# A fixed queue planned anew, with GpSimd left out of casts and copies of global values from tile 6 on

## The chip, the cores and the metric

The kernel runs on one core of a Trainium2 chip. The metric is the time of the device for one execution in microseconds (us), the median of several runs. An engine has its own queue and works through it in order: TensorE (PE in the profile; its weight loads are PEld), VectorE (DVE), ScalarE (ACT), GpSimd (POOL) and SyncE (SP), which here only issues DMA transfers.

## The reference: what is computed

Inputs are q, k and v of shape (4, 8, 768, 64), that is 4 batches, 8 heads, 768 positions and 64 columns, and four weights in float32. First comes attention with a narrow window, 96 local positions and 8 global ones, and then a feed-forward network (FFN) with three first matrices:

```python
scores = scale * q @ k.T                          # per batch and head
is_global = pos[None, :] < n_global               # 8
is_local = (rel >= 0) & (rel < n_local)           # 96, rel = query - key
bias = -slopes[h] * where(is_global & ~is_local, n_local, abs(rel))
a = softmax(where(is_global | is_local, scores + bias, -1e9))
x = (a @ v) as 3072 rows of 512                   # 4*768 rows, 8 heads * 64
h = maximum(maximum(x @ w1, x @ w2), x @ w3)      # 768 columns
out = h @ w_out                                   # 3072 x 512
```

## The kernel before

The 3072 rows are 24 *tiles* T of 128 rows, six per batch. A pair of tiles is a *group* G (256 rows), in which q, k and v are loaded. For the FFN the tiles form seven *chunks* of 4, 2, 2, 4, 4, 4 and 4 tiles, so a matmul has 512 or, in chunks 1 and 2, 256 columns.

Attention needs only the tile's own keys and those of the tile before it. The window is shorter than a tile, so the first rows of the tile before are free when it has been used as own tile, and the keys and values of the 8 global positions are copied into them: G(T) copies global keys, V(T) global values. V(T) stands behind the product of tile T that read these rows and ahead of the product of tile T+1. It has two halves, on partitions 0 to 3 and 64 to 67, one for even and one for odd positions.

All work is cut into *units*. A string, SCHEDULE, holds them in one order, and the kernel issues them one by one in that order; each engine thus gets its queue. A tile framework adds the semaphore waits where a unit reads what another wrote or takes a buffer that another used. A unit is a letter, its numbers, and, behind @, the buffer slot that it takes; where a unit may run on several engines the last number tells which: 0 ScalarE, 1 VectorE, 2 GpSimd, 3 a DMA. The letters:

- `l` a load of q (l0), k (l1) or v (l2) of a group, issued by SyncE (lines 213 and 220); group 12 stands for four tiles of batch 0 at once. `c` the cast of q or k to bfloat16 (L185), on GpSimd in two halves; `v` the cast of half a tile of v (L238). `w`, `W`, `q`, `Q` load and cast the FFN weights.
- `x`, `y` a transpose of q or k by TensorE (L252, L258) and its copy out of PSUM (L266, L269); `X` the same by a DMA transpose that SyncE issues (L274). `G` (L289, L291) and `V` (L302 on GpSimd, four-byte words; L304 on the others), as above.
- `S` the scores of four heads (L324; L316 adds the bias by a matmul where the unit's last number is 1), `e` the exponential (L331), `m` the multiplication by the mask and bias factor where S added no bias (L340; L342 for a batch's first tile), `A` the product with v (L366, L369) with the softmax sums as a 65th column, `n` the normalisation, a reciprocal and a multiplication (L377, L378). `B` and `K` write the eight heads' bias and mask tables from `R`.
- `t`, `u` the transpose of a normalised tile by TensorE (L393) and its copy (L396); `Z` the same by a DMA transpose (L399).
- `F` one FFN group c.f.j: four matmuls (L408) for chunk c, columns f (six times 128), matrix j. `f` takes it out of PSUM: j=0 a copy (L422, ScalarE or VectorE), j=1 a maximum (L424) and j=2 a maximum (L427), both on VectorE.
- `O`, `o`, `s` one output tile: six matmuls (L432), the copy out of PSUM (L447) and the store (L451). `E` is the last chunk's output (L437, L438). `D` are matmuls of zeros that fill waits at the start (L507).

PSUM has eight banks. F, O, t and x take one, S and A two, and the next unit on a bank waits until the last reader of the one before is done. So VectorE, which empties most banks, and TensorE are coupled both ways. The Vector, Scalar and Gpsimd units are picked from one table:

```python
copies = (nc.scalar.copy, nc.vector.tensor_copy, nc.gpsimd.tensor_copy)
```

The functions that the change touches, with their lines:

Of the kernel before, what the change touches and what calls it, by code (L numbers as in the profile page):

```python
# [586 lines left out]
```

## Time and profile before

| | us |
|---|---|
| median of 3 runs (lowest, highest) | 177.8 (176.94, 178.24) |
| profiled execution, whole | 177.18 |
| its span | 175.3 |
| TensorE busy in the span | 167.0 |
| VectorE, ScalarE, GpSimd busy | 133.9, 103.2, 43.9 |
| GpSimd: casts of v (26), copies of global values (20) | 14.2 and 3.2, 8.2 |
| GpSimd: casts of q and k (12 halves), of weights (8) | 7.3, 6.2 |
| first FFN matmul starts | 21.98 |

How to read it: the span runs from the first to the last instruction; 1.88 us lie around it. In a line of groups stand source line, engine, operation, output and inputs with shapes, count, then busy time, mean duration in ns, and the engine's idle time just before them with what ended it. Matmul durations overlap: a matmul of 512 columns is shown with 379 ns, and ten FFN groups of four take 8.74 us one behind another. In a line of the timeline stand start, duration, engine, source line and operation. Granted clock 1.00 is full speed. DMA share is the mean busy share of the DMA engines; in this profile it can exceed 1.

### The profile page before, as it was taken

The page shows a single profiled execution, that of the slowest core. Times are in us where ns is not written, and L with a number is a line of the kernel's source. Part 1 is how long each engine was busy: PE and PEld are TensorE (multiplying, and loading weights), DVE is VectorE, ACT ScalarE, POOL GpSimd, SP SyncE. Part 2 cuts the span into 40 slices and gives each one's busy share as a digit, 9 for nine tenths or more (in the row PEclk, how much of TensorE's full clock was granted, in tenths as well). Part 3 has the DMA queues.
Part 4 walks back from the last instruction along what each step waited for, and adds up shares of the span by engine and source line. Part 5 has one row for each costly group of instructions (what it writes and reads, how often), then busy time and mean ns, then how long its engine had stood idle before and what let it go on. Part 6 is the DMA issues. An engine that isn't in the chain of part 4 may idle for free.

```text
span 175.3 us, 3883 instructions
## 1 busy us (share of the span) xinstructions
PE 167.0 (95%) x1513; PEld 93.5 (53%) x1513; DVE 133.9 (76%) x264; ACT 103.2 (59%) x154; POOL 43.9 (25%) x86
## 2 busy tenths in 40 slices
PE   7599899999999999999999999999999999999992
PEld 2356644567967876544445545544444655444441
DVE  7689889898878988747998898949979985136840
ACT  5989776538979895664468967434216650250132
POOL 5139624536692423003002110160000110000000
PEclk9999999999999999999999999999999999999999
DMA  5999999999999969999999999999382173343006
GB/s 146 355 292 312 365 348 377 294 298 342 302 210 252 140 115 201 274 290 265 211 210 257 251 126 261 289 127 288 82 142 74 38 247 80 120 185 115 2 24 215
DMA packets 66082, 37.34 MB, mean 213 GB/s; under 512 B 24080, under 2 KB 60816, under 8 KB 66064
## 3 DMA queue, kind: packets, MB, share of 16 engines
q1 hardware_dynamic: 65920, 37.04, 84.3%
q8 instruction: 11, 0.18, 0.4%
q10 hardware_dynamic: 144, 0.07, 0.1%
q14 instruction: 7, 0.06, 0.1%
HBM read 25.17 MB, written 6.29 MB: 179 GB/s over the span
## 4 chain that ended last, share of the span: by engine, by line
PE 70%; DMA 9%; DVE 8%; ACT 4%; POOL 4%; issue 2%; SPq 2%; DVEq 0%; POOLq 0%
PE psum L408 47%; PE psum L432 13%; DMA rawqq<-in_q_dram 4%; PE psum L324 4%; DMA rawk<-in_k_dram 3%; PE psum L366 2%; PE psum L369 2%; POOL va L238 2%; DVE P L340 2%; DMA out_dram<-ost 2%; DVE h L424 1%; DVE xb L378 1%; ACT qb L185 1%; ACT P L331 1%; PE psum L258 1%
## 5 line engine op out<-in xcount | busy, mean ns | idle before, releaser
L408 PE MATMUL psum<-xT,w 128*128 128x512 bf16 (+1 forms) x504 | 99.7, 349 | 0.1
L408 PEld LDWEIGHTS <-w 128*128 128x128 bf16 x504 | 47.5, 98 | 43.0 <-issue 2.2
L331 ACT ACTIVATE P<-psum 128x1024 bf16<-128x1024 f32 (+1 forms) x48 | 43.2, 953 | 12.8 <-PE psum L324 12.8
L432 PE MATMUL psum<-wo,ht 128*128 128x512 bf16 (+2 forms) x156 | 33.8, 363 | 0.1
L424 DVE TENSOR_TENSOR h<-h,psum 128x512 bf16<-128x512 bf16 (+1 forms) x42 | 24.9, 605 | 5.5 <-PE psum L408 2.5
L427 DVE TENSOR_TENSOR ht<-h,psum 128x512 bf16<-128x512 bf16 (+1 forms) x42 | 26.2, 644 | 3.6 <-PE psum L408 2.6
L340 DVE TENSOR_TENSOR P<-P,wmask 128x1024 bf16<-128x1024 bf16 x36 | 25.4, 716 | 3.0 <-ACT P L331 2.3
L432 PEld LDWEIGHTS <-ht 128*128 128x128 bf16 x156 | 14.1, 98 | 14.0 <-DVE ht L427 0.5
L422 DVE CAST h<-psum 128x512 bf16<-128x512 f32 (+1 forms) x21 | 12.6, 610 | 11.2 <-PE psum L408 11.1
L422 ACT CAST h<-psum 128x512 bf16<-128x512 f32 (+1 forms) x21 | 10.7, 526 | 17.0 <-PE psum L408 15.4
L238 POOL CAST va<-rawv 64x512 bf16<-64x512 f32 x22 | 14.2, 648 | 21.8 <-DVE rz L377 11.3
L378 DVE TENSOR_TENSOR xb<-psum,rz 128x512 bf16<-128x512 f32 x24 | 16.6, 691 | 0.8
L324 PE MATMUL psum<-qkT 64*128 64x128 bf16 x352 | 14.9, 217 | 1.1 <-ACT qkT L266 0.7
L324 PEld LDWEIGHTS <-qkT 64*128 64x128 bf16 x352 | 10.3, 94 | 9.1 <-issue 6.0
L366 PEld LDWEIGHTS <-P 128*128 128x128 bf16 x192 | 12.5, 97 | 3.4 <-DVE h L424 0.9
L447 ACT COPY ost<-psum 128x512 f32<-128x512 f32 x14 | 7.9, 600 | 10.5 <-PE psum L432 10.3
L366 PE MATMUL psum<-va,P 128*128 128x65 bf16 x160 | 12.5, 193 | 0.4 <-DVE h L424 0.4
L238 ACT CAST va<-rawv 64x512 bf16<-64x512 f32 x14 | 8.7, 618 | 6.6 <-DMA rawv<-in_v_dram 6.4
L302 POOL COPY va<-vaf 4x260 int32<-4x260 int32 x20 | 8.2, 408 | 15.4 <-PE psum L369 12.5
L369 PEld LDWEIGHTS <-P 128*128 128x128 bf16 x160 | 10.4, 97 | 1.1
L369 PE MATMUL psum<-va,P 128*128 128x65 bf16 x128 | 9.9, 193 | 0.3 <-POOL va L302 0.3
L185 ACT CAST qb<-rawk 128x1024 bf16<-128x1024 f32 x6 | 6.3, 1052 | 6.0 <-DMA rawk<-in_k_dram 6.0
...
## 6 DMA issues: line engine op xcount, KB each, us to landing
rawv<-in_v_dram SPq DMA_DIRECT2D x12, 512.0 KB, 6.4
...
rawk<-in_k_dram SPq DMA_DIRECT2D x10, 512.0 KB, 6.5
rawq<-in_q_dram SPq DMA_DIRECT2D x10, 512.0 KB, 6.3
...
wst<-in_moe_w_dram SPq DMA_DIRECT2D x3, 512.0 KB, 7.9
wost<-in_moe_w_out_dram SPq DMA_DIRECT2D x3, 512.0 KB, 6.6
rawqk<-in_k_dram SPq DMA_DIRECT2D x2, 512.0 KB, 5.0
```

Of the source, the lines that this page charges most:

```text
L238: copies[how](heads(va(T))[64 * e:64 * e + 64, :, 0:D], src)
L324: nc.tensor.matmul(sp[:, hh, j2, ds], qT(T - ds, 1)[hsl, jp], qT(T, 0)[hsl, jp], start=not how, stop=True, skip_group_check=True)
L331: nc.scalar.activation(P[:, :, 0:n], sps[T, g].rearrange("p a b d n -> p (a b) d n")[:, :, 0:n], AF.Exp, bias=0.0, scale=scale)
L340: mul(P, P, wmask[:, g, :, 0:2])
L366: nc.tensor.matmul(o, P[:, i, 0], heads(va(T))[:, h], start=True, stop=(t == 0), skip_group_check=True)
L369: nc.tensor.matmul(o, P[:, i, 1], heads(va(T - 1))[:, h], start=False, stop=True, skip_group_check=True)
L378: nc.vector.tensor_tensor(out=x.rearrange("p (g h) d -> p g h d", g=2), in0=o4[:, :, :, 0:64], in1=rz[:, :, :, None].to_broadcast([128, 2, ...
L408: nc.tensor.matmul(ps, w123[f // 2][:, j, dm, (f % 2) * 128:(f % 2) * 128 + 128], xT[c][:, dm], start=(dm == 0), stop=(dm == 3))
L422: copies[how](h01, ps)
L424: nc.vector.tensor_max(h01s[c, f], h01s[c, f], ps)
L427: nc.vector.tensor_max(dst, h01s[c, f].rearrange("p (t e i) -> p t e i", e=2, i=64), ps.rearrange("p (t e i) -> p t e i", e=2, i=64))
L432: nc.tensor.matmul(po, ht[c][:, f, tt * 128:(tt + 1) * 128], wo[:, f, cols], start=(f == 0), stop=(f == NF - 1))
```

## The change

From tile 6 on no cast of q, k or v, no weight cast and no copy of global values is on GpSimd; these are on VectorE and ScalarE. The copies of global keys stay on it. V is two units now, one per half, and each may go to an engine of its own. The order of the queue is another one nearly everywhere: which chunk's groups come first, which tile is transposed by TensorE or by DMA, which evictions are on ScalarE, where the loads and stores stand, and which banks and slots each unit takes. Shapes, chunk sizes and numbers of buffers are unchanged. In the queue's text below, "..." marks parts left out; the parts shown are the start, the stretch from F1.0.0 to the first groups of chunk 3, and the entry of chunk 5.

```diff
 SCHEDULE = """
-    l1.12.1@0 l0.12.1@1 R B3.0 B1.1 l1.12.0@2 l0.12.0@3 K5 K3 K7 B4.2 B5.0 B0.0 B6.1 c1.12.1.1@0 B7.1 K6 K0
-    c0.12.1.1@1 B2.1 K4 c1.12.0.1 c0.12.0.1 l2.0.2@0 l2.1.2@1 D10.512@0 x12.1.1@0 D3.256@1 x12.0.1@1
-    y0.1.1.0@0 y0.0.1.0 S0.1.1@2 S1.1.0@4 l1.2.2@4 y1.1.1.0@1 l0.2.2@5 x12.1.0@0 y0.1.0.1 w0.1@0 e0.1@0
-    e1.1@1 y1.0.1.1 G0.2 w0.0@1 v1.1.1 D4.256@2 x12.0.0@2 y0.0.0.0 S1.0.1@4 G1.2 y1.1.0.0 e1.0@2 v0.0.2
-    S0.0.1@6 v0.1.2 w0.2@2 y1.0.0.1 v3.1.2 v2.1.2 S2.0.1@0 S2.1.0@2 G2.2 e0.0@3 w1.0@0 e2.0@4 m1.1.1 v1.0.1
-    A0@4 A1@6 e2.1@5 V1.2 l2.2.2@2 S3.0.1@0 n0@0 t0@4 v2.0.2 c1.2.2.0@2 e3.0@6 n1@1 S3.1.1@2 e3.1@7 t1@5
-    m2.1.1 v3.0.2 D2.256@6 A2@6 w1.1@1 V2.2 x2.1.2@0 c0.2.2.1 u1.1@0 x2.0.2@1 G3.2 n2@2 w1.2@2 l0.3.2@6
-    y2.1.2.0@2 y2.0.2.1 u0.0 W0.1.2 A3@2 W1.0.2 n3@3 t2@5 l1.3.2@0 u2.1 v5.0.2 S4.0.0@0 S4.1.0@6 G4.0 e4.0@0
-    D2.256@4 t3@4 u3.1 K1 K2 S5.0.0@2 W0.0.1 m4.0.1 W1.1.2 S5.1.0@0 l1.4.2@1 e5.0@3 e4.1@1 e5.1@2 F0.0.1@4
...
-    f1.2.0.0@0 f1.1.1.1 F1.0.0@0 F1.1.2@6 f1.1.2.1@1 f1.0.0.0@4 S6.0.0@2 c1.4.2.1@1 e6.0@4 S7.0.0@4 S7.1.0@0
-    e7.1@5 m6.0.1 S6.1.0@6 m7.1.1 l1.5.2@3 e6.1@6 l2.4.2@1 F0.4.2@2 F1.4.0@3 f1.4.0.0@2 l0.5.2@4 F1.0.1@0
-    F1.5.1@1 F1.4.1@3 F1.2.1@6 F1.5.0@7 e7.0@7 f0.4.2.1 f1.0.1.1 G6.0 F1.3.0@0 c0.4.2.0 G7.2 F1.3.1@2
-    f1.2.1.1 m7.0.1 F1.2.2@6 f1.3.0.0@3 c1.5.2.2@2 Q1.0 f1.5.0.1@1 l1.6.2@5 F1.0.2@0 A7@4 V7.2 v9.1.2
-    x4.1.2@7 v9.0.2 f1.3.1.1 m6.1.1 Q0.0 v8.0.2 f1.4.1.1 x4.0.2@2 F1.4.2@3 n7@2 f1.0.2.1 c0.5.2.2 v8.1.2
-    A6@4 O0.3@0 n6@3 f1.5.1.1 f1.4.2.1 f1.2.2.1 y4.1.2.0@0 y4.0.2.0 S8.0.0@4 S8.1.0@1 G8.1 e8.1@0 e8.0@1
-    O0.2@3 F1.5.2@1 t6@2 o0.2.0@0 m8.1.1 S9.0.0@4 f1.5.2.1 u6.1@2 Z7 m8.0.1 S9.1.0@6 G9.0 e9.1@2 O0.1@1
-    l2.5.2@2 e9.0@3 F2.0.0@2 A8@6 V8.2 m9.1.1 f2.0.0.0@4 F2.3.0@3 o0.1.0@0 F2.2.0@2 F2.5.0@1 m9.0.1 n8@0
-    l0.6.2@6 f2.5.0.1@2 f2.2.0.1@0 o0.3.0@1 f2.3.0.1@1 F2.3.1@0 f2.3.1.1 F1.3.2@4 c1.6.2.0@0 X10@1 F2.4.0@1
-    F2.2.1@5 c0.6.2.0 f1.3.2.1 A9@2 v10.1.0 f2.2.1.1 V9.2 f2.4.0.1@3 v11.0.2 S10.1.0@6 v11.1.2 S10.0.0@4
-    F2.4.1@0 O0.0@1 e10.1@5 X11 v10.0.0 G10.1 S11.1.0@6 Z8@0 n9@1 e10.0@7 f2.4.1.1 S11.0.0@2 e11.0@4
-    F2.5.1@0 m10.1.1 m10.0.1 F2.3.2@4 f2.3.2.1@0 F2.1.0@5 e11.1@6 A10@2 F2.2.2@4 m11.0.1 n10@2 f2.2.2.1
-    m11.1.1 F2.1.1@6 O1.0@7 X12@2 f2.1.0.0@1 V10.0 o1.0.0@1 o0.0.0@2 F2.4.2@2 f2.1.1.1 A11@4 f2.4.2.1 n11@3
-    O1.1@3 o1.1.0@2 l2.6.2@0 v12.0.1 f2.5.1.1 F2.5.2@1 f2.5.2.1 t11@2 u11.1 F2.1.2@0 S12.1.0@4 X13 Z9
-    e12.1@0 f2.1.2.1 S13.1.0@2 m12.1.1 S13.0.0@6 Z10 S12.0.0@0 e12.0@1 m12.0.1 e13.1@2 e13.0@3 l0.7.2@0
-    l1.7.2@1 F2.0.1@4 F3.5.0@5 F3.3.1@0 f2.0.1.1 v12.1.1 v13.1.2 l1.8.2@2 F3.3.0@1 l0.8.2@3 F2.0.2@4
-    c1.7.2.0@1 v13.0.2 c0.7.2.0 m13.1.1 f2.0.2.1 f3.3.0.0@0 F3.0.1@2 f3.5.0.0@3 l2.7.2@1 v14.0.0 F3.1.0@3
-    m13.0.1 f3.3.1.1 F3.3.2@4 A13@0 F3.2.0@5 f3.1.0.0@2 n13@0 F3.4.0@6 f3.4.0.1@1 c1.8.2.0@2 F3.4.1@7
...
-    F4.1.2@6 F4.0.1@5 c0.11.2.0@1 f4.0.1.1 l1.11.2@1 Z17 Z18 f4.0.2.1 Z19 F5.5.2@0 F5.1.0@3 F5.1.1@2
...
+    l0.12.1@0 l1.12.1@1 R K2 B3.1 K0 K1 K6 K3 B4.1 B2.1 B5.0 K5 K7 B0.1 B1.1 l1.12.0@2 c1.12.0.2@0 l0.12.0@3
+    B7.0 K4 c0.12.1.1@1 B6.1 D10.512@0 x12.0.1@0 l2.0.2@0 l2.1.2@1 c1.12.1.1 D3.256@1 x12.1.1@1 v1.0.2
+    y1.0.1.1@0 l1.2.2@4 l0.2.2@5 y0.0.1.0@1 y0.1.1.1 S1.1.1@2 c0.12.0.1 S0.1.0@4 D2.256@0 x12.1.0@0 w0.0@0
+    y1.1.1.0 e0.1@0 m0.1.1 D2.256@1 x12.0.0@1 y0.1.0.1 w0.1@1 w0.2@2 e1.1@1 y0.0.0.0 S1.0.1@2 v0.1.1
+    y1.1.0.0 G0.2 G1.2 w1.0@0 y1.0.0.1 S2.0.1@4 v1.1.2 e1.0@2 l2.2.2@2 S0.0.0@0 e0.0@3 w1.1@1 l1.3.2@6
+    w1.2@2 v0.0.1 v2.1.2 v2.0.2 m0.0.1 e2.0@4 D2.256@6 A1@2 V1.0.2 V1.1.2 n1@0 S2.1.1@0 G2.0 A0@4 S3.1.1@6
+    v3.1.2 S3.0.1@2 l0.3.2@0 e2.1@5 e3.1@6 v3.0.2 n0@1 c1.2.2.1@2 G3.2 A2@0 V2.0.2 V2.1.2 W0.0.2 x2.1.2@4
+    l2.3.2@0 c0.2.2.1 x2.0.2@5 t0@6 n2@2 e3.0@7 y2.0.2.1@2 A3@2 y2.1.2.0 n3@3 t1@4 u0.0@0 W0.2.2 S4.0.0@0
+    S4.1.0@6 G4.1 e4.0@1 t2@5 t3@2 u2.1 u1.0 D2.256@3 S5.0.0@0 u3.1 S5.1.0@2 e5.0@2 e4.1@0 e5.1@3 F0.1.0@4
+    W0.1.1 F0.1.1@5 F0.0.1@0 F0.0.0@1 f0.1.0.1@0 f0.0.0.0@1 W2.0.2 f0.1.1.1 m5.0.1 F0.1.2@2 F0.0.2@1 m4.0.1
...
+    F1.0.2@3 f0.2.1.1 F1.0.1@5 l0.4.2@1 c0.3.2.0 F1.0.0@4 F1.2.0@7 x3.1.2@0 y3.1.2.0@3 W1.2.1 f1.0.0.1@1
+    f0.3.1.1 v6.1.0 F0.2.2@1 f1.0.1.1 q2@0 q0@1 f0.5.1.1 f0.2.2.1 F1.1.0@2 l1.4.2@2 f1.2.0.0@0 F0.4.2@6
+    f1.0.2.1@1 x3.0.2@3 F0.5.2@7 y3.0.2.0 v6.0.0 v7.0.1 f0.4.2.1 F1.5.0@6 f1.5.0.0@1 f1.1.0.1@2 v7.1.1 q1@2
+    f0.5.2.1 F1.2.1@0 f1.2.1.1 S6.0.0@2 S7.0.0@4 e6.0@4 c0.4.2.1@1 S7.1.0@6 S6.1.0@0 e6.1@5 m6.0.1 e7.1@6
+    e7.0@7 F1.5.2@2 F1.5.1@3 m6.1.1 F1.4.0@0 F1.3.1@1 f1.4.0.0@3 f1.5.1.1 l2.4.2@1 F1.4.1@3 f1.5.2.1 A6@6
+    m7.1.1 F0.3.2@2 Q2.0 m7.0.1 x4.0.2@0 Q1.0 f1.4.1.1 A7@4 c1.4.2.0 F1.3.0@3 n6@2 F1.3.2@6 n7@3 f0.3.2.1
+    y4.0.2.1@1 f1.3.0.0@1 F1.1.2@7 v8.0.1 F1.4.2@4 f1.4.2.1 l1.5.2@3 l2.5.2@2 Z6@2 t7@2 F1.2.2@3 F1.1.1@0
+    f1.3.1.1 f1.2.2.1 f1.1.1.1 Q0.0 G6.2 l0.5.2@4 G7.0 x4.1.2@5 y4.1.2.0 u7.0 O0.2@4 V7.0.1 V7.1.1 v8.1.1
+    f1.1.2.1 f1.3.2.1 v11.1.1 S8.0.0@0 S8.1.0@2 G8.2 e8.1@0 m8.1.1 l1.6.2@5 e8.0@1 c1.5.2.1@2 l0.6.2@6
+    m8.0.1 O0.1@5 S9.1.0@2 e9.1@2 m9.1.1 S9.0.0@6 O1.1@0 c0.5.2.1 G9.1 o1.1.0@0 e9.0@3 F2.3.0@1 f2.3.0.1@4
+    l2.6.2@0 F2.5.0@2 f2.5.0.1@3 F2.0.0@0 f2.0.0.0@0 m9.0.1 o0.2.0@0 c1.6.2.0@0 F2.4.0@3 A8@6 O0.0@2 n8@1
+    V8.0.1 V8.1.1 v9.1.1 v10.0.1 v9.0.1 F2.5.1@4 f2.5.1.1 O0.3@0 A9@6 V9.0.1 V9.1.1 n9@0 c0.6.2.0 X10@0
+    o0.0.0@2 o0.1.0@1 o0.3.0@2 X11 f2.4.0.0@2 S10.0.0@4 X12@2 S10.1.0@0 F2.3.1@2 f2.3.1.1 l2.7.2@1 e10.0@4
+    G10.2 e10.1@5 F2.4.1@3 F2.3.2@4 Z9@0 m10.0.1 F2.1.0@2 f2.1.0.0@1 f2.4.1.1 v10.1.1 m10.1.1 S11.1.0@0
+    e11.1@6 S11.0.0@6 Z8 F2.1.1@5 f2.1.1.1 e11.0@7 f2.3.2.1@0 m11.1.1 O1.0@2 m11.0.1 v11.0.1 F2.2.2@3
+    S12.0.0@0 o1.0.0@1 X13 S12.1.0@4 e12.1@0 e12.0@1 A10@6 F2.0.1@2 V10.0.1 V10.1.1 F2.2.0@4 s0.1 n10@3
+    A11@0 n11@2 F2.2.1@5 f2.2.0.0@4 f2.0.1.1 F2.4.2@4 t10@6 F2.0.2@7 m12.1.1 u10.1 t11@2 l0.8.2@0 l1.7.2@1
+    F2.5.2@0 l0.7.2@2 F2.1.2@1 f2.1.2.1 v15.1.1 f2.4.2.1 f2.2.1.1 s0.0 c0.8.2.1@1 v14.0.0 u11.0 F3.1.0@2
+    F3.0.0@1 f3.0.0.1@1 G12.2 l1.9.2@3 f2.2.2.1 F3.0.1@6 F3.0.2@4 v14.1.0 v12.0.1 F3.2.0@5 F3.5.0@1 f2.5.2.1
+    F3.3.0@0 v13.1.0 f3.2.0.0@2 v13.0.0 F3.1.1@3 m12.0.1 F3.4.0@5 c1.7.2.1@2 f3.5.0.0@4 f3.0.1.1 v12.1.1
+    F3.4.1@1 f3.0.2.1@1 f3.4.0.0@3 f3.1.0.0@1 c0.7.2.1 f2.0.2.1 S13.1.0@4 S13.0.0@6 f3.4.1.1 f3.1.1.1
...
+    A19@6 F4.2.1@2 n17@0 n19@3 l2.11.2@2 F4.2.0@4 f4.3.1.1 Z16@2 A18@6 G18.0 f4.2.0.0@2 n18@2 F4.2.2@1
+    F4.0.1@4 F4.4.1@5 f4.0.1.1 f4.5.0.0@1 V19.0.1 V19.1.1 Z17 Z19 F4.0.2@0 F4.5.1@4 F4.3.2@6 f4.0.2.1 G19.1
+    Z18 F5.5.0@0 s3.0 l1.10.2@1 f4.2.1.1 F5.1.0@2 v22.1.0 c1.10.2.0@2 f5.5.0.0@3 f4.5.1.1 c0.10.2.1 f4.5.2.1
...
-LAST_BANKS = (3, 2, 4, 5, 1, 0, 7, 6)
-
-LAST_STAGES = ((1, 0, 2), (1, 0, 2))
+LAST_BANKS = (3, 7, 2, 6, 5, 4, 0, 1)
+
+LAST_STAGES = ((0, 2, 1), (2, 0, 1))
...
-    def u_V(slot, T, how):
+    def u_V(slot, T, e, how):
         b, t = divmod(T, NT)
+        rows = slice(64 * e, 64 * e + NG // 2)
         if how == 3:
-            dst, src = (va(x).rearrange("(e i) w -> e i w", e=2)[:, 0:NG // 2] for x in (T, b * NT))
-            nc.sync.dma_start(out=dst, in_=src)
-            return
-        for e in range(2):
-            rows = slice(64 * e, 64 * e + NG // 2)
-            if how == 2:
-                copies[how](words(va(T)[rows]), words(va(b * NT)[rows]))
-            else:
-                copies[how](va(T)[rows], va(b * NT)[rows])
+            nc.sync.dma_start(out=va(T)[rows], in_=va(b * NT)[rows])
+        elif how == 2:
+            copies[how](words(va(T)[rows]), words(va(b * NT)[rows]))
+        else:
+            copies[how](va(T)[rows], va(b * NT)[rows])
```

More of the change, by code (lines that the diff above doesn't have):

```diff
@@ new lines @@
+    f5.0.2.1 Z21@0 s4.1 S23.0.0@0 V21.0.0 V21.1.0 S23.1.0@2 e23.1@4 e23.0@6 m23.1.1 A22@6 V22.0.1 V22.1.1
+    n22@3 m23.0.1 O4.0@5 O5.0@4 O4.2@0 v23.1.0 o5.0.0@2 A23@2 O4.3@1 Z22 O5.1@4 Z20 O5.3@6 n23@2 Z23 O5.2@7
+    F6.4.0@2 o5.1.0@0 o4.3.0@2 s5.0 s4.3 f6.4.0.0@2 o4.0.0@0 o4.2.0@1 F6.1.2@1 o5.3.0@1 F6.1.0@4 F6.3.1@0
+    F6.2.0@5 F6.3.0@6 F6.3.2@2 f6.3.0.0@3 f6.1.0.1@0 f6.2.0.0@4 F6.1.1@3 f6.1.1.1 f6.3.1.1 f6.3.2.1@0
+    F6.0.2@6 F6.0.0@3 F6.2.1@0 s5.1 s4.0 F6.4.1@2 f6.4.1.1 F6.4.2@4 F6.0.1@2 F6.2.2@5 f6.0.0.0@1 f6.4.2.1
```

56 lines of the change are left out of this document (23 added, 33 removed).

## The prediction

> **What bounds the kernel now.** I read the page's first part, then a table by stretch, then the chain that ended last, then groups of instructions and the timeline. The first line is the page's; the others are the table's, their columns time, PE, PEld, DVE, ACT and POOL busy (instructions), granted clock, DMA share, GB/s.
> ```profile
> PE 167.0 (95%) x1513; PEld 93.5 (53%) x1513; DVE 133.9 (76%) x264; ACT 103.2 (59%) x154; POOL 43.9 (25%) x86
> ...
> 22.00:172.00 150.00, 149.23 (x1274) 82.65 (x1272) 116.50 (x218) 84.51 (x125) 32.55 (x60) 1.00 0.83 202
> ...
> 22.00:50.00 28.00, 27.96 (x260) 18.12 (x259) 25.05 (x46) 19.30 (x30) 15.05 (x24) 1.00 1.10 324
> ...
> 74.00:78.10 4.10, 3.73 (x22) 1.70 (x19) 1.83 (x4) 2.96 (x4) 0.00 (x0) 1.00 1.20 293
> ```
> From the first FFN matmul (21.98) to the last matmul (about 172) TensorE stands still for 0.77 us of 150, half of it (0.37) at 74 to 78, where ScalarE waits for a load. The clock is full. So nothing that frees another engine can shorten this part by more than 0.8; only the 22 us ahead of it, and new stalls, can move the time. In the first of these stretches VectorE is already busy for 25.05 of 28 us.
>
> The start is set by GpSimd. The chain there:
> ```profile
> 11.82 0.21 POOL qkT L291
> 12.04 0.56 POOL vaf L238
> ...
> 17.15 0.97 POOL va L238
> ...
> 18.61 0.41 POOL va L302
> 19.01 0.04 issue
> 19.05 0.19 PE psum L369
> ...
> 22.04 8.74 PE psum L408 x40
> ```
> Casts of v (L238) and copies of global values (L302) run one behind another until the A·v product of tile 3 may go on at 19.05; normalise, transpose and copy follow, then the FFN.
>
> **What moves, and its price.** From the groups with shapes kept apart:
> ```profile
> L238 POOL CAST va<-rawv 64x512 bf16<-64x512 f32 x22 | 14.2, 648 | 21.8 <-DVE rz L377 11.3 <-DMA rawv<-in_v_dram 9.7
> L302 POOL COPY va<-vaf 4x260 int32<-4x260 int32 x20 | 8.2, 408 | 15.4 <-PE psum L369 12.5 <-ACT P L331 2.2
> L238 DVE CAST va<-rawv 64x512 bf16<-64x512 f32 x4 | 2.0, 502 | 0.1
> L304 DVE COPY va<-vaf 4x520 bf16<-4x520 bf16 x6 | 1.7, 282 | 0.5 <-PE psum L369 0.4
> ```
> Counted in the queue: from tile 6 on GpSimd loses 18 casts of v, 6 of q or k (two halves each), 14 copies of global values, and one cast of w_out; its copies of global keys stay. VectorE gets 14 of the v casts at 0.38 (between the start of one and of the next where they follow each other; 0.42 alone), +5.3; 5 of the q and k casts at 0.61, +3.1; 14 copies at 0.30, +4.2; two PSUM copies at 0.61 and two bias rows at 0.35, +1.9. It gives up 7 first FFN evictions (five at 0.62, two at 0.34), -3.8, 5 output copies at 0.65, -3.3, and one weight cast, -0.7; two masks become small ones, -0.5. Net +6.2 of 128. ScalarE gains some 10. Behind the first FFN matmul all that is queued sums to 144 on TensorE, 118 on VectorE and 91 on ScalarE, so what counts is the place.
>
> (A) *The start.* The queue for the first 22 us is new too. GpSimd still has six v casts, four copies, and now three key copies, for one, among them ahead of tile 3's product, so the chain of 7.1 us (11.97 to 19.05) plus twice 0.21. It need not wait for a key copy first, and starts with the first v load, which is there by 11.27, when VectorE casts from it unhindered; the loads land 1.5 us apart and the fourth is cast at 9.35, so 11.1 or so. That is 18.6 in place of 19.05; the 0.3 for which the normalising of tile 3 waited for ScalarE (up to 19.77) shrinks, as ScalarE has a q/k cast less ahead of it. Taken: -0.8. If all six casts take the slowest 0.97 instead of the mean 0.83, +0.8, so a net +0.2, and +0.6 if the first load lands late; if GpSimd is not what ends last, ScalarE is: it reaches its last exponential of tile 3 about 0.7 sooner and product and copy could follow at once, -1.6.
>
> (B) *TensorE's own work.* Tile counts and matrices are the same; tile 10 is transposed by TensorE and no longer by DMA: four matmuls of 0.055, +0.2. The S units with bias matmuls and the warming matmuls lie in the start.
>
> (C) *The stretch that VectorE fills.* Between F1.0.0 and the transpose of tile 11 (t11) TensorE has 35 FFN groups (31 of 256 columns at 0.434, four of 512 at 0.863), six output tiles at 1.30, 14 S at 0.28 or 0.14, six A at 0.52 or 0.26, four transposes of q/k and two of x: 33.1, and 33.8 at the rate that the trace shows (149.2 for pieces that sum to 146.2). VectorE has there 24 second and third FFN steps (18 at 0.355, six at 0.64) 10.2, four first ones 1.4, ten masks at 0.605 and two at 0.345 6.7, six normalisations at 0.85 5.1, ten v casts 3.8, eight copies 2.4, three q/k casts 1.8, two more 0.8: 32.3, and 0.25 for two hand-overs. In the old queue the same landmarks hold 23.0 on VectorE against 28.9. So 1.3 us are left in which VectorE may stand still. In the stretch of before with 25.05 of 28 it stood still for 10.5%, unpressed; in its fullest five us (35 to 40) for 2.4%. Of 33.8 that is 0.8 to 3.5, so a stall of 0 to 2.2. Taken: 1.1, the middle, since it is pressed but its queue is in order.
> The copies add no wait: the normalisation behind them waits for the same product. The casts do: a cast on VectorE waits for its load with everything behind it. Such is c0.8.2.1. Its load l0.8 stands on SyncE behind Z9, Z8, X13 and a store. Between the end of n9, which frees Z9, and the landing lie three transposes at 1.23, a store at 0.58, and 6.3:
> ```profile
> rawq<-in_q_dram SPq DMA_DIRECT2D x10, 512.0 KB, 6.3
> ...
> xT<-xb SPq DMA_TRANSPOSE x15, 4.2
> ```
> 10.6 us; VectorE has 9.4 of work in between, so it waits 1.2. TensorE's first group that needs what lies behind is F3.3.0 (its bank is emptied by f2.5.2): 15.3 after A9, with VectorE there at 14.6. A landing of more than 7.0 becomes a stall; those of q range from 4.6 to 11.9, a stall of 0 to 4.9. Taken: 0.3.
>
> (D) *The entry of chunk 5.* Between A18 and F5.5.0 TensorE has six groups, 5.3 us. Normalisation (0.25 and 0.85) and the transpose Z18 (4.2; 2.4 to 6.1) take 5.3 too. Old: seven groups, 6.2. Stall 0 to 1.9; taken 0.3. The last entry, Z23 before chunk 6, has the same 5.3 in both queues, and the end, 18 groups and four output tiles, is the same work: 0.
>
> (E) *Stalls that go.* At 74.8 ScalarE cast a k that had landed 6.06 us after its issue (c1.7), and two evictions of chunk 3 stood behind it. Now VectorE casts it, after l0.8, and its place is six FFN groups later: -0.4 of the 0.77 (0 to -0.8).
>
> VectorE's durations above are clean ones. Why may they be:
> ```profile
> 43.30 1.09 DVE L340 TENSOR_TENSOR P<-P,wmask 128x1024 bf16<-128x1024 bf16 x1
> ...
> 99.18 0.68 DVE L340 TENSOR_TENSOR P<-P,wmask 128x1024 bf16<-128x1024 bf16 x1
> ...
> 43.05 1.81 POOL L185 CAST wo<-wost 128x512 bf16<-128x512 f32 x2
> ```
> The same masking takes 1.09 while GpSimd casts and 0.68 when it doesn't. From tile 6 on such excesses sum to about 2 us in before, and in the new queue nothing causes them. [...]
>
> **Sum.** -0.8 + 0.2 + 1.1 + 0.3 + 0.3 - 0.4 = +0.7. The profiled execution took 177.18 (span 175.3 and 1.88 around it): 177.9. It lies 0.6 below the median of the runs shown, so against 177.8 the forecast is 178.5, +0.4%, under the 1% (176.0 to 179.6) that a measurement here can tell from nothing.
>
> **Rivals.**
> *VectorE becomes the bound (slower).* Place: F1.0.0 to F3.3.0. For: 32.5 of 33.8 needed, an in-order queue with casts that wait for loads. Against: TensorE's eight banks give some lead, and VectorE kept up at 97.6% over five us. It decides from 1.3 us of VectorE idle, and from a landing of l0.8 above 7.0. At the 10.5% of before, (C) is 2.2, and one late landing (8 us) adds 1.0: 177.8 + 0.7 - 1.4 + 3.2 = 180.3.
> *The start counts, and nothing stalls (faster).* (A) at -1.6, (C) and (D) nothing, (E) -0.4: 177.8 - 1.6 + 0.2 - 0.4 = 176.0, at best 175.6. For: the 2 us of excess gone. Against: 0.77 is all the stall that there was.
> *The change is not there:* the new queue has only key copies on GpSimd from tile 6 on, so I give it nothing.
>
> **Chances.** Forecast (176.0 to 179.6) 0.52; VectorE the bound 0.34; the start alone, below 176.0, 0.14. These are also same, slower and faster. Range 175.8 to 181.6: from near the best case to the forecast with (C) at 2.2 and the load 2.0 later.
>
> **What would show it.** (A) The first FFN matmul at 21.2 (20.4 to 22.6). (B) TensorE's busy time about 167 again. (C) VectorE busy over 94% between F1.0.0 and t11, and TensorE there idle for about a microsecond, waits of PE naming L424 or L427; c0.8.2.1 waiting for rawq. (D) A wait for a DMA transpose at the first group of chunk 5. Masking never above 0.75 behind tile 6. Wrong it would be by a stall that no line of before shows: a load that an in-order ScalarE waits for (v16.0.0 behind l2.8, c1.10 behind Z18), or a start in which ScalarE's eight mask exponentials, now ahead of its first copies, end last.

## The result and the profile after

| | before | after |
|---|---|---|
| median of four runs each, us (lowest, highest) | 177.56 (176.94, 178.24) | 179.75 (179.62, 181.49) |
| profiled execution, whole, us | 177.18 | 179.74 |
| its span, us | 175.3 | 177.5 |
| first FFN matmul starts, us | 21.98 | 21.98 |
| last matmul ends, us | 171.9 | 174.2 |

After over before is 1.0131, with a 95% interval of 1.0086 to 1.0177. The changed kernel is slower by 1.3%, and the two profiled executions, 2.56 us apart, say where.

The first line below is the page's of after; the others are from its table by stretch (time; PE, PEld, DVE, ACT and POOL busy with instructions; granted clock, DMA share, GB/s). In this kernel most source lines stand two lines higher: an FFN matmul is L406, the product with v L364 and L367, V is L302, o is L445 and a store L449, and the cast of v is L239.
```profile
PE 169.1 (95%) x1517; PEld 93.8 (53%) x1517; DVE 137.0 (77%) x288; ACT 113.9 (64%) x172; POOL 16.6 (9%) x39
...
22.05:174.30 152.25, 149.93 (x1276) 82.90 (x1276) 119.62 (x239) 95.22 (x143) 5.55 (x13) 1.00 0.81 198
...
105.00:115.40 10.40, 8.61 (x88) 4.79 (x87) 8.48 (x17) 6.41 (x13) 0.00 (x0) 1.00 1.24 280
115.40:131.00 15.60, 15.60 (x74) 6.82 (x70) 12.24 (x22) 6.54 (x10) 0.00 (x0) 1.00 0.83 202
```
The second line begins 0.07 us late and runs 0.1 us past the last matmul. From the start of the first FFN matmul to the end of the last matmul TensorE's stretch is 152.22 us, 2.25 longer than before. Busy time is 0.75 more (150.00 against 149.25), idle time 1.5 more (2.22 against 0.72), and 1.79 of the idle time lies in one stretch, 105.0 to 115.4, the first products of chunk 4. The view of waits of the same kernel gives it one line (engine, line, whom it waited for; total, times, longest):
```profile
PE psum L367 <- ACT va L302: 1.8, 1, 1.8
```
TensorE waits for a copy of global values, V16, on ScalarE. V16 is one of the units that the change took from GpSimd. But the chain that ended last, followed back from there, does not end at V16 (start, duration, what):
```profile
103.28 6.07 DMA out_dram<-ost
...
109.43 0.59 ACT ost L445
...
110.04 0.63 ACT va L302
...
110.69 0.63 ACT va L302
...
111.36 0.19 PE psum L367
```
V16 stands on ScalarE behind the output copy `o3.0.0@2`, and that copy waits 1.8 us for a store to leave its buffer. Slot 2 of that staging buffer still holds tile 6's output, whose store s2.0 is issued at 103.28 and is done 6.07 us later. Why so late, the timeline of SyncE shows (start, duration of the issuing, line, what, how many):
```profile
95.59 3.53 SPq L397 DMA_TRANSPOSE xT<-xb  x2
99.16 0.57 SPq L449 DMA_DIRECT2D out_dram<-ost  x1
99.78 3.39 SPq L221 DMA_DIRECT2D rawv<-in_v_dram  x3
103.28 1.72 SPq L449 DMA_DIRECT2D out_dram<-ost  x1
```
In the new queue s2.0 stands behind two transposes (Z12, Z14), another store and the three loads l2.8, l2.9 and l2.10. In the kernel before, tile 8's output copy was on VectorE and V16 on GpSimd, so neither stood ahead of the other.

### The profile page after: what moved, and what is told of

The parts are those of the page before. It is cut to its first block, busy times and chain, and to the rows that moved or that the text cites. A ratio compares the mean times of both kernels' runs of the same rounds, so it can differ in the third digit from the quotient of the medians.

```text
span 177.5 us, 3857 instructions
## 1 busy us (share of the span) xinstructions
PE 169.1 (95%) x1517; PEld 93.8 (53%) x1517; DVE 137.0 (77%) x288; ACT 113.9 (64%) x172; POOL 16.6 (9%) x39
## 4 chain that ended last, share of the span: by engine, by line
PE 76%; DMA 10%; DVE 7%; ACT 3%; issue 1%; SPq 1%; DVEq 0%; ACTq 0%
PE psum L406 47%; PE psum L430 16%; PE psum L322 6%; DMA rawqq<-in_q_dram 4%; DMA out_dram<-ost 3%; PE psum L364 3%; DMA qkT<-qb 3%; PE psum L367 2%; DVE ht L425 1%; ACT P L329 1%; PE psum L391 1%; DVE qb L186 1%; PE psum L259 1%; SPq L214 1%; DVE h L422 1%
## 5 line engine op out<-in xcount | busy, mean ns | idle before, releaser
L406 PE MATMUL psum<-xT,w 128*128 128x512 bf16 (+1 forms) x504 | 99.7, 349 | 0.1
L406 PEld LDWEIGHTS <-w 128*128 128x128 bf16 x504 | 47.4, 98 | 42.5 <-issue 1.4
L420 ACT CAST h<-psum 128x512 bf16<-128x512 f32 (+1 forms) x28 | 14.3, 526 | 17.7 <-PE psum L406 17.6
L338 DVE TENSOR_TENSOR P<-P,wmask 128x1024 bf16<-128x1024 bf16 x34 | 23.0, 696 | 1.0 <-ACT P L329 0.7
L445 ACT COPY ost<-psum 128x512 f32<-128x512 f32 x19 | 10.7, 598 | 8.7 <-PE psum L430 6.6
L420 DVE CAST h<-psum 128x512 bf16<-128x512 f32 (+1 forms) x14 | 8.4, 609 | 9.7 <-PE psum L406 9.5
L364 PEld LDWEIGHTS <-P 128*128 128x128 bf16 x192 | 12.4, 97 | 4.3 <-issue 1.9
L364 PE MATMUL psum<-va,P 128*128 128x65 bf16 x160 | 12.6, 193 | 0.0
L367 PE MATMUL psum<-va,P 128*128 128x65 bf16 x128 | 9.9, 193 | 1.8 <-ACT va L302 1.8
L367 PEld LDWEIGHTS <-P 128*128 128x128 bf16 x160 | 10.5, 97 | 1.8 <-issue 0.4
L292 POOL COPY qkT<-kg 128x32 bf16<-128x32 bf16 x7 | 1.9, 272 | 96.5 <-PE psum L322 96.3
L239 ACT CAST va<-rawv 64x512 bf16<-64x512 f32 x16 | 9.9, 618 | 0.4
L375 DVE RECIPROCAL rz<-psum 128x8 f32<-128x8 f32 x24 | 4.9, 203 | 5.6 <-PE psum L367 4.7
```

Of the source, the lines that this page charges most:

```text
L338: mul(P, P, wmask[:, g, :, 0:2])
L364: nc.tensor.matmul(o, P[:, i, 0], heads(va(T))[:, h], start=True, stop=(t == 0), skip_group_check=True)
L367: nc.tensor.matmul(o, P[:, i, 1], heads(va(T - 1))[:, h], start=False, stop=True, skip_group_check=True)
L406: nc.tensor.matmul(ps, w123[f // 2][:, j, dm, (f % 2) * 128:(f % 2) * 128 + 128], xT[c][:, dm], start=(dm == 0), stop=(dm == 3))
L420: copies[how](h01, ps)
L445: copies[how](osts[c, tt], pos[c, tt])
```

## The experiments

Theory 1: the place of that store, with what stands behind it on ScalarE, is the loss. Theory 2, a rival: copies, casts and masks on VectorE have made it the bound, and the wait merely shows where its delay comes out. A third stood in the prediction: the start counts.

The measured numbers of all twelve (median; ratio to the kernel before on the same chip, with its interval; span, first FFN matmul and end of the last matmul of the profiled execution; TensorE's idle time from 105 to 116):

| | us | ratio | span | first FFN | last matmul | idle 105 to 116 |
|---|---|---|---|---|---|---|
| before | 177.56 | | 175.3 | 21.98 | 171.9 | 0.17 |
| after | 179.75 | 1.0131 (1.0086 to 1.0177) | 177.5 | 21.98 | 174.2 | 1.79 |
| e1 | 178.81 | 1.0078 (1.0039 to 1.0117) | 176.5 | 22.01 | 173.2 | 0.86 |
| e2 | 178.59 | 1.0046 (1.0016 to 1.0075) | 177.1 | 21.67 | 173.4 | 1.27 |
| e3 | 179.81 | 1.0131 (1.0066 to 1.0195) | 177.5 | 21.44 | 174.0 | 1.78 |
| e4 | 199.84 | 1.1249 (1.1182 to 1.1315) | 198.1 | 21.86 | 194.3 | 1.74 |
| e5 | 179.94 | 1.0114 (1.0047 to 1.0181) | 176.9 | 21.80 | 173.1 | 0.63 |
| e6 | 179.34 | 1.0091 (1.0026 to 1.0155) | 177.0 | 21.48 | 173.4 | 0.99 |
| e7 | 179.00 | 1.0065 (1.0000 to 1.0131) | 178.0 | 21.96 | 174.7 | 1.19 |
| e8 | 179.44 | 1.0090 (1.0027 to 1.0154) | 177.6 | 21.90 | 174.2 | 0.92 |
| e9 | 179.47 | 1.0098 (1.0059 to 1.0137) | 177.6 | 21.95 | 174.3 | 0.05 |
| e10 | 180.53 | 1.0149 (1.0117 to 1.0181) | 177.8 | 21.98 | 174.5 | 0.16 |
| e11 | 179.08 | 1.0059 (1.0033 to 1.0085) | 177.8 | 21.60 | 173.9 | 0.05 |
| e12 | 177.96 | 1.0011 (0.9984 to 1.0039) | 176.1 | 21.95 | 172.6 | 0.02 |

Three cautions for reading it. In the traces of e1 to e4 and e9 to e11, 21 or 22 of some 1,515 matmul records are missing (all weight loads are there), and each leaves a hole of about 0.05 us that counts as idle; in these, the named waits say more than the sum. The kernels with the start of after begin the FFN at 21.67 to 22.01, so a few tenths of a microsecond between two single executions decide nothing.

And the time around the span is a property of the kernel here. It is 2.2 to 2.4 us in every run of after, e1, e3, e5, e6, e9 and e10, and 1.7 to 2.0 us in every run of e2, e4, e7, e8, e11 and e12; before has medians of 1.80 to 1.85. No view shows what lies there. So 0.4 to 0.5 us of the 2.2 us that the changed kernel lost is in none of the waits below, and when two kernels of different sorts are compared (e5 and e12, e1 and e2, e9 and e11) about half a microsecond of the difference of their times is this.

### e1: the store earlier

```diff
-    u15.1 S19.1.0@0 e19.1@0 Z14 o3.1.1@2 s0.2 S19.0.0@4 ...
+    u15.1 S19.1.0@0 e19.1@0 Z14 o3.1.1@2 s0.2 s2.0 S19.0.0@4 ...
...
-    s2.0 A16@4 o3.0.0@2 ...
+    A16@4 o3.0.0@2 ...
```


> The changed queue with one unit moved: the store s2.0 right behind s0.2, ahead of the three v loads l2.8, l2.9, l2.10 that it stood behind. Theory 1 (the loss is one wait: the output copy o3.0 on ScalarE waits for its buffer, which s2.0 was still sending, and the copies V16 behind it hold up the product of tile 17 for 1.8 us): s2.0 lands before 104, ScalarE has no wait for out_dram at o3.0, TensorE's idle time behind the first FFN matmul falls from 2.3 to about 0.6, time 178.0 (177.6 to 178.4). Theory 2 (VectorE and ScalarE are too full, the wait would only show elsewhere): 179.3 to 179.8.

The ratio fell from 1.0131 to 1.0078 and the span by 1.0. The wait for V16 and o3.0's wait for the store are gone from the trace. Half of the gain is lost again, in a wait and a chain that were not there (view of waits of PE, then the chain, of e1):
```profile
PE psum L406 <- ACT h L420: 0.8, 1, 0.8
```
```profile
101.39 4.57 DMA rawv<-in_v_dram
...
105.98 0.62 ACT va L239
106.60 0.49 ACT h L420
...
107.13 1.02 PE psum L406 x4
```
The load l2.8 now stands one store further back on SyncE. ScalarE waits for it with the cast v16.0, and the FFN copy f4.1.0 behind that cast keeps F4.1.2 from its bank. The place in the queue is not all of that: with the store in its old place the same cast waits 0.9 us in e2 and 1.0 us in e7, and hardly at all in after and e3, so this load lands about when it is needed. So theory 1 holds for the wait, but the store was not the whole of it, and the time lies between the two theories.

### e2: V16 back on GpSimd, the store where it is

```diff
-    ... V16.0.0 V16.1.0 ...
+    ... V16.0.2 V16.1.2 ...
```


> The changed queue with the two copies V16 back on GpSimd, everything else in place; o3.0 still waits for its buffer. Theory 1 (the wait reaches TensorE only through V16 on ScalarE): the product of tile 17 starts about a microsecond behind that of tile 16 and the FFN groups between, ScalarE still waits 1.8 us for out_dram, TensorE does not, time 178.0 (177.6 to 178.5). Rival (ScalarE standing still is felt anyway, through f4.3.0 and the v casts behind it): TensorE waits 1 us or more at a later place of chunk 4, 178.9 to 179.7.

The product of tile 17 no longer waits. But o3.0 still waits 1.81 us for the store (timeline of ScalarE), and the FFN copy f4.3.0 behind it is now what TensorE waits for, 0.5 us. With the 0.7 us for f4.1.0, behind v16.0 and its late load, that makes 1.2 us (waits of PE):
```profile
109.88 0.59 ACT L445 COPY ost<-psum 128x512 f32<-128x512 f32 x1 [1.81 <-DMA out_dram<-ost]
```
```profile
PE psum L406 <- ACT h L420: 1.2, 2, 0.7
```
The rival's second wait was there, though at half of its price. That ScalarE stands still is felt either way; who stands behind it decides which line shows it and how much of the 1.8 us reaches TensorE. The lower time of e2 against e1 (178.59 against 178.81) is no merit of this edit: its spans are longer (median 176.85 against 176.55), and the difference lies around them.

### e5: the store earlier, and the FFN copy ahead of the cast

```diff
-    ... l2.8.2@2 v16.0.0 f4.1.0.0@3 v16.1.0 ...
+    ... l2.8.2@2 f4.1.0.0@3 v16.0.0 v16.1.0 ...
```
with e1's edit.

> The store s2.0 early as in e1_store_early, and ScalarE does the FFN eviction f4.1.0 before the v cast v16.0.0, so that the eviction no longer stands behind the load l2.8. Theory (the new time of the changed kernel is these two waits on ScalarE, one uncovered by removing the other): TensorE's 0.8 us wait for h goes, the stretch 105 to 116 has under 0.3 us idle, and the time is 0.8 us under that of e1_store_early: 178.0 us, 0.2 to 0.4% above the kernel before. Rival (the trouble only moves to the next unit on ScalarE, since l2.8 lands as late and V16 and o3.0 follow the same cast): 178.6 to 179.0 us, with 0.6 us or more idle between 105 and 116.

TensorE's wait for h went, but 0.5 us of the wait for V16 came back. ScalarE's timeline in e5 shows why (in brackets the idle time before an instruction and what ended it):
```profile
106.05 1.26 ACT L239 CAST va<-rawv 64x512 bf16<-64x512 f32 x2 [0.50 <-DMA rawv<-in_v_dram]
107.86 0.62 ACT L239 CAST va<-rawv 64x512 bf16<-64x512 f32 x1 [0.54 <-DMA rawv<-in_v_dram]
```
It waits for l2.8 and for l2.9. The last matmul ends where e1's does. The rival was right: the trouble moved to the next unit. The median, 179.94, is even above what the rival expected, and the profiled execution (179.19) is the fastest of the four; what made the others slower was not traced.

### e9: the load l2.8 earlier

```diff
-    ... Z13@1 X19 S16.0.0@2 ...
+    ... Z13@1 X19 l2.8.2@2 S16.0.0@2 ...
```
with e5's edit, l2.8 removed from its old place.

> e5_store_early_evict_first with the load l2.8 issued behind X19, ahead of the transposes Z12 and Z14 and the stores (its buffer has been free since tile 11's casts). On SyncE it goes out at some 95.6 us in place of 101.4, so that it lands by 100 to 101 and v16.0 on ScalarE (106.0 in e5, after 0.5 us of waiting) waits no more. Theory (what is left of the new stall in e5 is this landing): idle time of TensorE between 105 and 116 falls from 0.63 to under 0.2 us, the span from 176.9 to 176.4, the time by 0.5. Rival 1 (Z12 and Z14 now go out 0.6 to 1.7 us later and chunk 4 begins later): a new wait of TensorE for xT ahead of F4.3.0, and the span 177 or more. Rival 2 (DMA is full there, so l2.9 lands later instead and v19.0 takes v16.0's place as the one that waits): idle 0.4 to 0.6 and the span 176.8 as before.

The load was there in time: v16.0 no longer waits, and 105 to 116 is filled. But Z14 lands at 104.3 in place of 102 or so, and the first group of chunk 4 waits. The timeline of TensorE's weight loads in e9:
```profile
102.11 0.45 PEld L322 LDWEIGHTS <-qkT 64*128 64x128 bf16 x16
104.28 2.72 PEld L406 LDWEIGHTS <-w 128*128 128x128 bf16 x14 [1.72 <-DMA xT<-xb]
```
(The view of waits puts this stall down to a VectorE copy; that had long been done, and the weight load names the transfer.) Rival 1 was right, and the span rose to 177.6. Store early, the cast's load late; load early, the transpose late: whatever goes first on SyncE, something behind it is late. That points to a queue that is full, and not to a unit in a wrong place.

### e12: one transpose off SyncE

This run tries it by taking work off the queue and leaving its order: tile 12 is transposed by TensorE, and VectorE, which stands still for 2 us there, copies it.
```diff
-    ... o2.0.0@2 A14@0 ...
+    ... o2.0.0@2 t12@7 u12.1@1 A14@0 ...
...
-    ... Z13@1 X19 ...
+    ... Z13 X19 ...
...
-    ... t15@3 Z12 u15.1 ...
+    ... t15@3 u15.1 ...
```
with e5's edit.

> e5_store_early_evict_first with tile 12 transposed by TensorE (t12 ahead of A14, its copy u12 on VectorE, which stands still there for 2 us) in place of Z12. Theory (what is left of the stall at 105 to 111 is the queue of SyncE, which issues without a pause from 81.4 to 107.2 in e5, seven transposes of q/k and x ahead of the load l2.8 among it, whereas e9 only changed who in it is late): one issue of 1.2 to 1.9 us less, Z14 lands no later than in e5 (102.1), s2.0 and l2.8 are issued 1.2 to 1.9 us sooner (l2.8 at 99.5 to 100.2 in place of 101.4), v16.0 on ScalarE waits 0 in place of 0.5 us, and TensorE's idle time between 105 and 116 falls from 0.63 to under 0.25 us; TensorE pays 0.22 us for the transpose. Span 176.9 less 0.2 to 0.4, time 178.4 to 179.0. Rival (the landing of l2.8 is set by the transfers, which are full from 100 on, and not by when it is issued): v16.0 waits 0.4 us or more and idle stays above 0.5 us; the span is 177.1.

The time is 177.96 us and the ratio 1.0011 (0.9984 to 1.0039): the loss can no longer be told from nothing. SyncE in e12 (the first two lines) now has a pause of 1.7 us after 95.60, where in after it issued without one from 81.4 to 107.2 (in e5, to which the expectation ascribes these figures, from 81.3 to 107.6); and ScalarE casts v16 at 105.52, right behind the copy before it:
```profile
94.28 1.32 SPq L275 DMA_TRANSPOSE qkT<-qb  x1
97.34 1.20 SPq L397 DMA_TRANSPOSE xT<-xb  x1
...
100.78 2.80 SPq L221 DMA_DIRECT2D rawv<-in_v_dram  x3
```
```profile
105.05 0.62 ACT L420 CAST h<-psum 128x512 bf16<-128x512 f32 x1
105.52 1.27 ACT L239 CAST va<-rawv 64x512 bf16<-64x512 f32 x2
```
```profile
105.00:116.00 11.00, 10.98 (x99) 5.91 (x97) 9.72 (x20) 7.84 (x15) 0.00 (x0) 1.00 1.28 246
...
21.95:172.57 150.62, 150.11 (x1283) 83.24 (x1280) 119.91 (x240) 94.94 (x142) 5.82 (x13) 1.00 0.82 200
```
The load was issued only 0.6 us sooner than in e5 (100.78 against 101.41), less than the 1.2 to 1.9 that were expected, and that was enough, since only 0.5 was missing. TensorE stands still for 0.5 us in all behind the first FFN matmul, less than the 0.7 of before. The rival, that the transfers and not their issue set the landing, is out for l2.8; for l2.9 ScalarE still waits 0.4 us, but no wait of TensorE comes of it.

What is shown is that the stall in chunk 4 hangs on SyncE's queue: TensorE's idle time there went from 0.63 us in e5 to 0.02. That is less than the 1.8 us between the two ratios. Half a microsecond of these lies around the span (2.3 us in e5, 1.8 in e12), and of the rest the traces show little, as the profiled execution of e5 is the fastest of its four. Nor is it shown that the transpose alone would do, as e12 also has e5's two other moves.

### e3, e6 and e11: the start

Half of tile 2's v cast goes from GpSimd to VectorE:
```diff
-    w1.2@2 v0.0.1 v2.1.2 v2.0.2 ...
+    w1.2@2 v0.0.1 v2.1.1 v2.0.2 ...
```


> The changed queue with one v cast of the start (tile 2, second half) on VectorE, which is idle from 12.7 to 13.9, and no longer on GpSimd. Theory 1 (GpSimd's chain of casts and copies sets the start): tile 3's product goes on at 18.2 in place of 18.9, the first FFN matmul starts at 21.4 (21.2 to 21.7) in place of 22.05, time 0.6 shorter, 179.1. Rival (ScalarE's and VectorE's own queue between that product and the FFN set it): the first FFN matmul at 21.9 or later, 179.5 to 179.9.

> The edit of e5_store_early_evict_first together with that of e3_v2_vector (half of tile 2's v cast on VectorE). Theory (in e3 the 0.55 us won at the start were eaten on the way, 0.2 by a transpose by DMA that tile 10 waits for at 62 and 0.25 by VectorE at 91, and the rest by the store that lands when it lands): with the store early the last 0.2 us survive, 177.8 us against 178.0 for e5. Rival 1 (only the store ate it): the full 0.55 us come through, 177.45. Rival 2 (nothing comes through): the same as e5 within 0.1, 178.0.

The edit does what it should at the start: tile 3's product goes on at 18.43 in place of 18.86 (timelines), and the first FFN matmul starts at 21.44, 0.54 us sooner. GpSimd has one cast less ahead of its last copies, and the transposes ahead of that product (L259, 16 matmuls) take 1.05 us in place of 1.29. In after the chain comes to them from VectorE's casts, the last of which, c0.2, takes 1.11 us beside GpSimd's casts, which end at 17.40; in e3 it comes from TensorE's own work. The time does not move (179.81 against 179.75). In the traces of after (first fence) and e3 (second) a lead of 0.54 us has become 0.35 by the scores of tile 10, which need a DMA transpose:
```profile
57.72 5.10 DMA qkT<-qb
...
62.86 0.62 PE psum L322 x16
```
```profile
57.19 5.27 DMA qkT<-qb
...
62.51 0.62 PE psum L322 x16
```
At 92 it is 0.1, after a wait for VectorE at 91; the last matmul ends 0.2 us sooner, within what single executions differ by. With e5's edit (e6), in which the store holds up nothing, the FFN begins 0.3 us sooner than in e5, and the last matmul ends 0.3 us later. The median is 0.6 below e5's, but the intervals overlap widely (1.0091 and 1.0114), so it is not shown that anything comes through.

e11 takes e9 and adds e2's and e3's edits:

> e9_l28_early with V16 on GpSimd (as in e2_v16_gpsimd) and half of tile 2's v cast on VectorE (as in e3_v2_vector). Theory (every stall that the new order brought has been taken out, what is left against the kernel before is some 0.7 us more of TensorE's busy time): first FFN matmul 21.45, idle behind it 0.8 us, span 175.9, time 178.2, 0.2 to 0.5% above the kernel before. Rival (the start's gain is eaten on the way by waits at 62 and 91, as in e3): span 176.3, time 178.6. Faster than the kernel before it is by neither.

It has e9's stall for Z14 again (1.5 us), at 179.08 us 0.4 below e9, with intervals that overlap; the spans have the same median (177.2), so the 0.4 lies around them. The forecast of 178.2 had taken e9's stall for mended.

### e4 and e7: order and engines apart

e4 is the kernel before with its queue in the old order, and the 32 units only moved to other engines; e7 is the changed kernel's order with the old engines. A few of the tokens, e4 first:
```diff
-    ... v6.1.2 ... v6.0.2 ... c1.5.2.2@2 ... V7.2 ...
+    ... v6.1.1 ... v6.0.1 ... c1.5.2.1@2 ... V7.1 ...
```


> The old queue in its old order with only the engines changed: from tile 6 on the 18 casts of v on GpSimd go to VectorE (14) and ScalarE (4), the six casts of q and k and the seven copies of global values to VectorE, the w_out cast to ScalarE. VectorE gets 14 us more and gives nothing. Theory 1 (TensorE bounds the kernel and VectorE has room, but casts that wait for loads, in the queue ahead of evictions, stop TensorE): 178.5 to 181 and waits of TensorE for VectorE of 1 to 3 us. Rival (TensorE is the bound and nothing else is felt): 177.0 to 178.0. Rival 2 (VectorE becomes the bound): over 182.

```diff
-    ... c1.3.2.0@0 ... v6.1.0 ... V7.0.1 V7.1.1 ... V16.0.0 V16.1.0 ...
+    ... c1.3.2.2@0 ... v6.1.2 ... V7.0.2 V7.1.2 ... V16.0.2 V16.1.2 ...
```


> The counterpart of e4_old_order: the new queue, but 17 casts of v, 6 of q and k and the copies of global values of ten tiles are put back on GpSimd, and the copy Q2 too. Theory (the engines by themselves are worth little, the order must fit them): GpSimd gets back some 26 us of work, VectorE and ScalarE lose some 17 between them, A17's wait goes with V16 on GpSimd, masks are slower beside GpSimd's casts (1.0 against 0.7 us, ten of them: 3 us of VectorE's time); 178.5 to 181 us, with new waits of TensorE for va or qb cast by GpSimd. Rival 1 (VectorE is the bound of the changed kernel between 36 and 72 and the engine move is what costs): 177.0 to 177.8, below the changed kernel by 1%. Rival 2 (the order is tied to its engines as closely as the old one was, where the mismatch cost 20 us): above 185.

The move of engines alone costs 22 us (199.84). The theory expected 178.5 to 181; of the size only the rival that VectorE becomes the bound (over 182) had an idea. Its longest wait of TensorE, in the timeline and the chain of e4:
```profile
43.69 0.58 PE L410 MATMUL psum<-xT,w 128*128 128x512 bf16 x1 [5.89 <-DVE h L426]
```
```profile
34.34 6.17 DMA rawv<-in_v_dram
...
40.54 0.42 DVE va L240
...
41.43 0.69 DVE h L426
```
A cast that GpSimd could wait with alone now makes VectorE wait for a load, and the FFN maxima behind it are late. VectorE is busy for less of the span than in after (73% against 77%), so it is waiting, not work, that costs. In the new order most of these casts stand where their loads have landed. So the new order, with the evictions that it takes from VectorE, gives back some 20 of the 22 us.

e7 puts 18 casts of v, six of q and k, the copies of seven tiles and one weight cast back on GpSimd (its expectation says 17 and ten tiles). It is 179.00, 1.0065 (1.0000 to 1.0131), as its theory had it. Its interval overlaps that of after, so the old engines in the new order are not shown to be better or worse; its spans have a median of 177.25, against 177.45 in after, so most of what it is faster by lies around them. The same store holds up o3.0 there (chain of e7), and TensorE waits for h three times, once (0.4 us) behind it (waits of PE, e7):
```profile
104.19 5.80 DMA out_dram<-ost
...
110.06 0.58 ACT ost L445
```
```profile
PE psum L406 <- ACT h L420: 1.9, 3, 0.8
```
So the store's place, which is part of the order, holds up ScalarE with either set of engines. What the engines decide is what stands behind it.

### e8: less on VectorE

```diff
-    ... V7.0.1 V7.1.1 ... V8.0.1 V8.1.1 ... V15.0.1 V15.1.1 ...
+    ... V7.0.2 V7.1.2 ... V8.0.2 V8.1.2 ... V15.0.2 V15.1.2 ...
```
with e5's edit, and likewise for tiles 9, 10, 13 and 14.

> e5_store_early_evict_first, with the copies of global values of tiles 7 to 10 and 13 to 15 back on GpSimd, which takes 2.0 us of VectorE's 33.3 in the stretch 36 to 72 and 1.4 more up to 105. Theory (VectorE has work without end there but TensorE hardly waits for it): no gain, 178.0 us as e5, within 0.2. Rival (VectorE is the bound: its 94% in that stretch sets the pace): 0.3 us less, which is all that TensorE stands still there, 177.7 us. It would be slower than e5 by over 0.5 us only if a copy on GpSimd holds up the product that waits for it.

The stretch that VectorE fills, in e5 (first) and e8:
```profile
36.80:72.30 35.50, 34.99 (x409) 25.05 (x407) 33.15 (x77) 28.58 (x43) 1.01 (x4) 1.00 1.02 236
```
```profile
36.80:72.30 35.50, 34.86 (x404) 24.86 (x402) 30.93 (x69) 28.86 (x43) 4.00 (x12) 1.00 1.09 235
```
VectorE has 2.2 us less to do, and TensorE stands still for 0.64 in place of 0.51 us. The time is the same within the intervals, and so is the span (medians 177.65 and 177.65). Theory 2 is out.

### e10: tile 10 transposed by DMA, as before

```diff
-    ... t10@6 F2.0.2@7 m12.1.1 u10.1 ...
+    ... Z10 F2.0.2@7 m12.1.1 ...
```
with e9's edit.

> e9_l28_early with tile 10 transposed by DMA (Z10 in place of t10 and u10.1), as in the kernel before. Theory (step B): TensorE's busy time behind the first FFN matmul falls by 0.2 us (four matmuls of 0.055), VectorE loses one copy of 0.4, and the span falls by 0.2. Rival (step C: the cast of l0.8 on VectorE waits 0.7 us already, and Z10 puts 1.2 us more on SyncE ahead of that load): VectorE waits 1.9 us there and TensorE stands still for 0.3 to 1.2 us more between 60 and 76; the span rises by as much less 0.2.

The time is 1.1 us above e9's, and the intervals of the two ratios overlap only a little (1.0098, up to 1.0137, and 1.0149, from 1.0117). The rival's sign was right, but not its mechanism: no wait of TensorE (waits of PE, e10) names the cast of l0.8, which waits 0.7 us in after. What TensorE waits for is Z10 itself, which lands late for chunk 3 (timeline of PE in e10):
```profile
73.86 6.42 PE L406 MATMUL psum<-xT,w 128*128 128x512 bf16 x28 [0.79 <-DMA xT<-xb]
```

## Why the prediction was right, and where it was not

The time, 179.75, lies in the range of 175.8 to 181.6 and 1.25 above the forecast of 178.5. Of the three cases it belongs to "slower by over 1%", if only just and with an interval that reaches down to 0.9%; that had 0.34, and within 1% had 0.52. That it lies in the range is luck in part: the range reached that far because of the stall in (C), and that stall did not come. Against its own base, 177.18 and +0.7, the profiled execution came out at +2.56. By the steps of the sum:

- **(A) the start, -0.8:** 0, the first FFN matmul starts at 21.98 in both. GpSimd's casts and copies end sooner, and tile 3's product went on at 18.88, 0.17 sooner than before and not 0.45. But GpSimd was not alone in setting that: TensorE itself came to this product at 18.69 and waited 0.2 us for the last copy, and the chain that ended last goes by two casts of q and k on VectorE, c1.2 and c0.2, and the transposes behind them. In before c1.2 was on ScalarE; the step counted only what ScalarE lost. And what was won was lost behind the product. The chain of after:
```profile
16.33 1.63 DVE qb L186 x2
...
18.01 0.62 PE psum L259 x8
...
18.88 0.17 PE psum L367
...
19.82 0.41 DVE xb L376
...
20.43 0.52 DVE qkT L292
20.95 0.66 DVE xT L394 x2
...
21.65 0.40 PE psum L322 x8
22.05 0.97 PE psum L406 x4
```
  Between the normalisation of tile 3 and the copies u2 and u3 VectorE now does the key copy G4 (0.52), which was on ScalarE. The step took for given that "product and copy could follow". And e3 shows that the term would have been worth little even at its size: 0.54 us won there left the time where it was.
- **(B) TensorE's own work, +0.2:** +0.75. The four matmuls of tile 10 were right; the other 0.5 are in busy time that is modelled from pipelined matmuls, and e5 to e8 and e12 have as much or more (0.6 to 1.1 above before), though e7 runs on the old engines. So it belongs to the order; what in it is not settled. TensorE's whole busy time is 169.1 and not about 167; the rest of that lies in the start, 19.1 us against 17.8 ahead of the first FFN matmul, and cost no time. That the transpose by TensorE is nothing to regret is shown by e10.
- **(C) the stretch that VectorE fills, +1.4 with its late load:** about +0.25. The picture was right and the price too high. From 36.4 to 72.0 VectorE was busy for 94% of the time and TensorE stood still for 0.32 us; the cast of l0.8 waited 0.7 us, and no TensorE wait came of it:
```profile
36.40:72.00 35.60, 35.28 (x409) 25.29 (x408) 33.33 (x77) 29.22 (x43) 0.84 (x4) 1.00 1.00 238
```
  An in-order engine at 94% need not hold up another: what it lacks is slack for a wait, and here none was long enough. The rival that VectorE becomes the bound names a time (180.3) close to what came, by a mechanism that did not happen.
- **(D) the entry of chunk 5, +0.3:** 0. TensorE fills 115.4 to 131.0 to the last 0.01 us.
- **(E) the stall at 74 to 78, -0.4:** as forecast, it is gone.
- **Masks:** none above 0.75 behind tile 6, as said, with a mean of 0.684 from 55 us on in after against 0.762 in e7, where GpSimd casts again: 2.2 us over 28 masks. In before the mean there is 0.689, and three long masks stand ahead of 55: 0.83, 1.09 and 1.02 us at 42.54, 43.30 and 52.74, each beside a cast on GpSimd. The same shapes take 0.42 and 0.68 elsewhere (and 0.42 also at 47.30, beside a cast). These three give 1.2 of the about 2 us that the prediction counted; that the rest is gone is not shown. That it brought no time is what e8 says too: VectorE's work was not what ended last.

What failed is a term that was not in the sum: the entry of chunk 4. The prediction looked at an entry of that kind in (D), for chunk 5, and counted SyncE's queue in (C), ahead of l0.8; it did neither for the stretch from 81 to 107 us, where SyncE issues without a pause, and it compared no output copy with the store that empties its buffer. Its last paragraph did name the neighbour, "a load that an in-order ScalarE waits for (v16.0.0 behind l2.8, ...)"; ScalarE's wait is real in e1, e2, e5 and e7 (0.5 to 1.0 us), but in the traced execution of the changed kernel the load had landed when ScalarE came to the cast. The 2.56 us between the two executions are 0 at the start, 0.75 of busy time, -0.3 of idle time elsewhere (C, D and E together), 1.79 for this stall, -0.05 behind the last matmul and 0.36 around the span (2.24 against 1.88), which no view shows. A to E together thus came to +0.45, not far from the forecast +0.7, by errors that cancel.
